# Packed-key products in float32 on 64-by-32 tiles, and weights kept in one float32

## Chip, cores and metric

The kernel runs on one core of one Trainium2 chip. The metric is the device time of one execution in microseconds (us).

## What is computed

Eight batches of eight heads pass through two softmax attentions (576 queries, 32 packed positions, head size 64), then two feed-forward layers follow on 4608 tokens. q, k, v and p are float32; all weight matrices are float64. Cut to what matters:

```python
def sm_attn(qq, kk, vv):                       # per batch and head
    s = scale * np.matmul(qq, kk.transpose(0, 1, 3, 2))
    s = s - np.max(s, axis=-1, keepdims=True)
    a = np.exp(s)
    a = a / (np.sum(a, axis=-1, keepdims=True) + 1e-09)
    return np.matmul(a, vv)
p_packed = sm_attn(p, k, v)                    # [8, 8, 32, 64]
out = sm_attn(q, p_packed, p_packed)           # [8, 8, 576, 64]
x = out.transpose(0, 2, 1, 3).reshape(4608, 512)
h = np.maximum(np.maximum(x @ w1, x @ w2), x @ w3)   # [4608, 768]
x = h @ w_out                                        # [4608, 512]
h = x @ w_in                                         # [4608, 2048]
P = a[0] + a[1] * h + a[2] * h**2 + a[3] * h**3
Q = 1.0 + abs(b[0]) * abs(h) + abs(b[1]) * h**2
result = (P / (Q + 1e-06)) @ w_out2                  # [4608, 512]
```

## The kernel before

**Stages.** Batches are worked in four pairs (`bp`). A pair has four units `u`: a batch (`b2`) and a group of four heads (`g`). For a unit, `s_stage` (S) multiplies p with k, `a_stage` and `v_stage` (T, V) form the packed values, `z_stage` (Z) transposes them into `ppk`, the packed keys. `s2_stage` (s) multiplies them with q; two later softmax steps (g) give `a2h` and `a2l`, the second attention's weights. The second attention's values meet w1, w2 and w3 first: `m_stage` (m) multiplies packed keys by a piece of these weights, and `y_stage` multiplies the result `mh`, `ml` by `a2h`, `a2l`, for each of six blocks `f` of 128 hidden columns and each of three weights `w`, and keeps the maximum `hm`, which becomes `hh`, `hl`. `x2_stage` multiplies these by `w_out` and stores x to HBM. When all four pairs are done, a last part (`h_mm`, `g_stage`, `o_mm`) does the rational layer in nine blocks of 512 tokens.

**High and low parts.** Most products are done as three fp32r products of high and low parts (`mm3`, lines 61 to 63). `split` (lines 51 to 58) casts to the high part on ACT and subtracts on DVE or POOL. The score products (lines 260 and 322) and those of line 363 are float32 products, each with 32 columns of the array, written to a quarter of PSUM's partitions; `pt` and `ppk` hold zeros in the rows of the other head, so that all 128 rows take part.

**Weights.** A float64 weight comes as two 32-bit words per element. `decode` takes it apart on DVE, ACT and POOL into `hi` and `lo`. `Feed` hands out the pieces: `step()` finishes the piece begun before, begins the next and loads a further one into `w_raw` (three buffers). 24 pieces of 384 columns (w1, w2, w3) and six of 512 (w_out) are decoded in START and in the first pair and stored to `w_scr`, from where `again` loads them for the later pairs. 32 pieces of 512 (`w_2`, for the last part) are decoded in pairs 1 to 3.

**Order.** `START` is a list written by hand for pair 0: each `|` ends a step, F is `feed.step()`, L, W and l load k, v and q. In `y_stage`, `between()` runs after each of the 36 groups of 12 products of a pair: it starts m stages of the next f, one step of `PACK` (the next pair's S, T, V, Z) and a feed step. `SECOND` runs between the x2 stages. A scheduler then places the instructions of each engine in an order of its own that follows the program's as its priority. All loads named here go through SyncE's queue, in order.

## Time and profile before

| | |
|---|---|
| median of 3 runs | 1428.18 us (1426.24 to 1429.65) |
| the profiled execution | 1429.64 us |
| its span, first to last instruction | 1427.9 us |
| mean granted TensorE clock | 0.973 |

The profile is of one execution. Busy time is the time in which an engine ran instructions; PEld is the weight load that overlaps PE's products. The granted clock is a share of full speed. A float32 product of 32 columns leaves two records in the profile (x16 for eight products). Matmul ends are modelled, so the distance from one start to the next is the safer measure.

### The profile page before, as it was taken

Reading aid. Unit: us, or ns where it says so; the run is one execution under the profiler, and the core shown is the slowest. Engines: PE = TensorE matmul, PEld = TensorE weight load, DVE = VectorE, ACT = ScalarE, POOL = GpSimd, SP = SyncE. Lnnn points to the kernel's source line nnn. Section 1 sums busy time; section 2 is a strip of 40 time slices with the busy share of each in tenths; the row PEclk is TensorE's granted clock in tenths of the full one; section 3 lists DMA queues with packets and bytes.
Section 4 is the critical chain, followed back from the end, with each engine's and each line's share of the span. In section 5 each row is a group of like instructions: output and inputs, shape, how many; then the busy total and the mean of one; then the engine's idle time right before and its main releaser. Section 6 shows DMA issues by size and latency. Waiting matters only on the chain.

```text
span 1427.9 us, 21290 instructions
## 1 busy us (share of the span) xinstructions
PE 1337.6 (94%) x8016; PEld 1140.2 (80%) x8016; DVE 1093.5 (77%) x1712; ACT 893.0 (63%) x1523; POOL 351.1 (25%) x350
## 2 busy tenths in 40 slices
PE   5468899998999899999999999999999999999998
PEld 2257799887988799998888888888888888888886
DVE  5999854668475848339897888978888888888887
ACT  4577743655355536337686766868677686676765
POOL 4676632447444555300010100101001010000000
PEclk9598999999999999999999999999999999999999
DMA  9757662768556645583010100101001010010000
GB/s 290 224 188 220 221 232 78 245 209 297 173 174 228 240 165 192 180 293 154 1 59 1 56 4 7 53 1 60 1 8 52 1 52 1 11 42 0 31 1 30
DMA packets 76743, 159.72 MB, mean 112 GB/s; under 512 B 11104, under 2 KB 35680, under 8 KB 75872
## 3 DMA queue, kind: packets, MB, share of 16 engines
q1 hardware_dynamic: 76352, 157.84, 33.0%
q8 instruction: 63, 1.03, 0.3%
q10 hardware_dynamic: 288, 0.52, 0.1%
q14 instruction: 40, 0.33, 0.1%
HBM read 113.25 MB, written 45.09 MB: 111 GB/s over the span
## 4 chain that ended last, share of the span: by engine, by line
PE 76%; DMA 7%; DVE 3%; ACT 2%; issue 1%; SPq 0%; POOL 0%; DVEq 0%; ACTq 0%; POOLq 0%
PE po L61 9%; PE po L63 9%; PE po L62 9%; PE psh L62 9%; PE psh L61 9%; PE psh L63 9%; PE psy L61 6%; PE psy L63 6%; PE psy L62 6%; DMA w_raw<-in_w_dram 3%; DMA wi_b<-w_scr 2%; DMA w_scr<-wt 1%; DVE wt L88 1%; PE pst L363 1%; DVE ml L58 1%
## 5 line engine op out<-in xcount | busy, mean ns | idle before, releaser
L619 ACT ACTIVATE hb<-psh,babs 128x512 f32<-128x512 f32 (+1 forms) x145 | 100.1, 690 | 190.0 <-PE psh L63 190.0
L61 PE MATMUL po<-wq_b,gh 128*128 128x512 f32 x540 | 212.3, 393 | 0.8 <-ACT gh L54 0.8
L62 PE MATMUL po<-wq_b,gh 128*128 128x512 f32 x540 | 211.3, 391 | 0.0
L61 PE MATMUL psy<-a2h,mh 128*128 128x288 f32 x576 | 179.9, 312 | 31.3 <-ACT hm L449 13.8
L62 PE MATMUL psh<-xl,wi_b 128*128 128x512 f32 x504 | 196.9, 391 | 0.0
L63 PE MATMUL psh<-xh,wi_b 128*128 128x512 f32 x504 | 196.6, 390 | 0.0
L61 PE MATMUL psh<-xh,wi_b 128*128 128x512 f32 x504 | 196.5, 390 | 0.0
L58 POOL TENSOR_TENSOR xl<-xr,xh 128x512 fp32r<-128x512 f32 x28 | 36.5, 1304 | 627.7 <-ACT xh L54 627.7
L622 DVE SCALAR_TENSOR_TENSOR hb<-h,babs,hb 128x512 f32<-128x512 f32 (+1 forms) x145 | 108.3, 747 | 98.1 <-ACT h L620 98.0
L63 PE MATMUL po<-wq_b,gl 128*128 128x512 f32 x540 | 181.7, 391 | 0.0
L63 PE MATMUL psy<-a2h,ml 128*128 128x288 f32 x576 | 173.3, 301 | 2.5 <-DVE ml L58 2.4
L62 PE MATMUL psy<-a2l,mh 128*128 128x288 f32 x576 | 172.8, 300 | 0.0
L61 PEld LDWEIGHTS psy<-a2h,mh 128*128 128x128 f32 x576 | 110.9, 193 | 43.2 <-ACT hm L449 17.2
L61 PE MATMUL psy<-hh,wo_h 128*128 128x288 f32 x384 | 115.9, 302 | 9.6 <-ACT hm L467 8.6
L63 PEld LDWEIGHTS po<-wq_b,gl 128*128 128x128 f32 x540 | 101.3, 188 | 24.0
L61 PEld LDWEIGHTS po<-wq_b,gh 128*128 128x128 f32 x540 | 101.4, 188 | 22.9 <-ACT gh L54 1.2
L62 PEld LDWEIGHTS po<-wq_b,gh 128*128 128x128 f32 x540 | 101.4, 188 | 22.5
L451 DVE TENSOR_TENSOR hm<-psy,hm 128x576 f32<-128x576 f32 x96 | 72.4, 754 | 58.3 <-PE psy L63 54.6
L63 PE MATMUL psy<-hh,wo_l 128*128 128x288 f32 x384 | 115.0, 299 | 0.0
L62 PE MATMUL psy<-hl,wo_h 128*128 128x288 f32 x384 | 114.9, 299 | 0.0
L621 ACT ACTIVATE u<-psh,av 128x512 f32<-128x512 f32 (+1 forms) x145 | 113.9, 785 | 1.6 <-DVE gl L58 1.6
L627 DVE SCALAR_TENSOR_TENSOR u<-u,av,h 128x512 f32<-128x512 f32 (+1 forms) x145 | 107.8, 743 | 8.3 <-ACT h L624 8.3
(114 smaller groups left out, 3203.4 us busy)
## 6 DMA issues: line engine op xcount, KB each, us to landing
wt<-w_scr SPq DMA_DIRECT2D x72, 384.0 KB, 4.4
w_raw<-in_w_dram SPq DMA_DIRECT2D x32, 512.0 KB, 5.0
w_scr<-wt SPq DMA_DIRECT2D x32, 512.0 KB, 4.3
kt<-in_k_dram SPq DMA_DIRECT2D x16, 576.0 KB, 5.2
vraw<-in_v_dram SPq DMA_DIRECT2D x16, 576.0 KB, 6.7
w_raw<-in_w_dram SPq DMA_DIRECT2D x24, 384.0 KB, 3.4
kt<-in_q_dram SPq DMA_DIRECT2D x16, 576.0 KB, 6.7
w_scr<-wt SPq DMA_DIRECT2D x24, 384.0 KB, 3.4
```

The lines of the kernel that those rows point to most:

```text
L58: e.tensor_tensor(out=lo, in0=src, in1=hi.bitcast(F32), op=ALU.subtract)
L61: pe.matmul(out_ap, lhsT=lh, rhs=rh, start=first, stop=False)
L62: pe.matmul(out_ap, lhsT=lh, rhs=rl, start=False, stop=False)
L63: pe.matmul(out_ap, lhsT=ll, rhs=rh, start=False, stop=last)
L88: dve.scalar_tensor_tensor(out=hib, in0=hw, scalar=-0x80000000, in1=t, op0=ALU.bitwise_and, op1=ALU.bitwise_or)
L363: pe.matmul(pv[32 * h : 32 * h + 32, :64], lhsT=at[:, 3 * i + cp, o : o + 32], rhs=vt[:, h, c, :], start=c == 0, stop=c == VC - 1)
L451: dve.tensor_tensor(out=hm, in0=ps[:, :, :288], in1=hm, op=ALU.max)
L619: act.activation(hb, h, AF.Abs, scale=babs[:, 0:1])
L621: act.activation(u, h, AF.Identity, scale=av[:, 3:4], bias=av[:, 2:3])
L622: dve.scalar_tensor_tensor(out=hb, in0=h2, scalar=babs[:, 1:2], in1=hb, op0=ALU.mult, op1=ALU.add)
L627: dve.scalar_tensor_tensor(out=u, in0=u, scalar=av[:, 0:1], in1=h2, op0=ALU.add, op1=ALU.mult)
```

## The change

- **m products.** `m_stage` no longer uses fp32r parts on 128 rows and 128 columns. Per head it issues one float32 product of 64 rows by 32 columns, 384 wide; eight per stage, with all three weights of a group of heads in one stage. The evacuation is one split of 128 partitions instead of two of 64. `pp` goes, and with it most of `z_stage`.
- **Scores.** Both score products take the 64 rows of their own head; the zeros go.
- **Weights.** Pieces of w1, w2, w3 are 768 wide, twelve in number, and are kept in one float32 (`single`). The low word is added on DVE instead of ACT and POOL, for all pieces. w_out comes as four pieces by its output columns. `half_step` does half of `step`; a piece is now loaded when another is finished, and Feed2 starts with three loaded.
- **Order.** START is rewritten, with six half steps and two softmax steps left for the y stage; `between` starts m stages one step later (2 and 4 of 6 instead of 1 and 3) and takes 22 half steps in pair 0; x2 runs over output blocks outside and batches inside. `hl` of pair 0 (and the last of each pair) is subtracted on DVE. The coefficients a and b are loaded in the last pair. The first block of the last part's weights has a tile of its own, `wi_0`, and the second moves to `wi_b`.

```diff
@@ -65,76 +65,90 @@
...
-    def decode(pl, raw, n):
+    def decode(pl, raw, n, single):
         hw, lw = raw[:, :, 1], raw[:, :, 0].bitcast(U32)
-        t = pl.tile([128, n], I32, name="dec_t", bufs=2)
-        r = pl.tile([128, n], I32, name="dec_r", bufs=2)
-        rf = r.bitcast(F32)
-        dve.tensor_scalar(out=t, in0=hw, scalar1=0x7FFFFE00, scalar2=None, op0=ALU.bitwise_and)
-        dve.tensor_scalar(out=r, in0=hw, scalar1=0x1FF, scalar2=None, op0=ALU.bitwise_and)
+        t = pl.tile([128, 768], I32, name="dec_t", bufs=2)[:, :n]
+        r = pl.tile([128, 768], I32, name="dec_r", bufs=1)[:, :n]
+        keep = 0x7FF00000 if single else 0x7FFFFE00
+        dve.tensor_scalar(out=t, in0=hw, scalar1=keep, scalar2=None, op0=ALU.bitwise_and)
+        if single:
+            dve.tensor_scalar(out=r, in0=hw, scalar1=0xFFFFF, scalar2=0x100000, op0=ALU.bitwise_and, op1=ALU.bitwise_or)
+        else:
+            dve.tensor_scalar(out=r, in0=hw, scalar1=0x1FF, scalar2=None, op0=ALU.bitwise_and)
         act.activation(t, t, AF.Relu, scale=8.0, bias=reb)
-        mixed = next(plans) == "m"
-        if mixed:
-            dve.scalar_tensor_tensor(out=rf, in0=lw, scalar=2.0**-32, in1=r, op0=ALU.mult, op1=ALU.add)
+        act.activation(r.bitcast(F32), r, AF.Copy, scale=2.0**-20)
+        hi, lo = yield
+        rf = lo if single else r.bitcast(F32)
+        dve.scalar_tensor_tensor(out=rf, in0=lw, scalar=2.0**-52, in1=r.bitcast(F32), op0=ALU.mult, op1=ALU.add)
+        hib = hi if hi is not None and hi.dtype == I32 else t
+        dve.scalar_tensor_tensor(out=hib, in0=hw, scalar=-0x80000000, in1=t, op0=ALU.bitwise_and, op1=ALU.bitwise_or)
+        if single:
+            w = t
         else:
-            l = raw[:, :, 0].bitcast(F32)
-            act.activation(l, lw, AF.Copy, scale=2.0**-52)
-            act.activation(rf, r, AF.Copy, scale=2.0**-20)
-            pool.tensor_tensor(out=rf, in0=rf, in1=l, op=ALU.add)
-        hi, lo = yield
-        hib = hi if hi.dtype == I32 else t
-        dve.scalar_tensor_tensor(out=hib, in0=hw, scalar=-0x80000000, in1=t, op0=ALU.bitwise_and, op1=ALU.bitwise_or)
-        w = pl.tile([128, n], I32, name="dec_w", bufs=1)
-        dve.tensor_scalar(out=w, in0=hib, scalar1=-0x00800000, scalar2=None, op0=ALU.bitwise_and)
-        if mixed:
-            dve.tensor_scalar(out=w.bitcast(F32), in0=w.bitcast(F32), scalar1=2.0**-20, scalar2=None, op0=ALU.mult)
-        if hib is t:
-            act.copy(hi, t.bitcast(F32))
+            w = hw
+            dve.tensor_scalar(out=w, in0=hib, scalar1=-0x00800000, scalar2=None, op0=ALU.bitwise_and)
+            if hib is t:
+                act.copy(hi, t.bitcast(F32))
         pool.tensor_tensor(out=lo, in0=rf, in1=w.bitcast(F32), op=ALU.mult)
...
     class Feed:
+        def __init__(self, pl, pieces, bufs, first=0):
             self.pl, self.pieces, self.bufs, self.raw, self.half = pl, iter(pieces), bufs, [], []
-            self.load()
+            for _ in range(first):
+                self.load()
-        def step(self):
+        def start(self):
+            if self.raw:
+                raw, piece = self.raw.pop(0)
+                gen = decode(self.pl, raw, raw.shape[1], piece[3]) if wide else None
+                if gen is not None:
+                    next(gen)
+                self.half.append((gen, raw, piece))
+        def finish(self):
             if self.half:
-                gen, raw, (tiles, _, then) = self.half.pop(0)
+                gen, raw, (tiles, _, then, single) = self.half.pop(0)
                 hi, lo = tiles()
...
                         pass
+                elif single:
+                    act.copy(lo, raw)
...
-            if self.raw:
-                raw, piece = self.raw.pop(0)
-                gen = decode(self.pl, raw, raw.shape[1]) if wide else None
-                if gen is not None:
-                    next(gen)
-                self.half.append((gen, raw, piece))
                 self.load()
+        def half_step(self):
+            if self.half:
+                self.finish()
+            else:
+                self.start()
+        def step(self):
+            self.finish()
+            self.start()
...
@@ -146,62 +160,66 @@
...
-    w_scr = dram.tile([6, NHP, 128, 2, 384], F32, name="w_scr")
+    w_scr = dram.tile([6, 2, 128, 768], F32, name="w_scr")
     w2_scr = dram.tile([128, 2, 32 * 512], F32, name="w2_scr")
...
-    wo_h = big_b.tile([128, 6, DM], F32R, name="wo_h")
-    wo_l = big_b.tile([128, 6, DM], F32R, name="wo_l")
+    wo_h = big_b.tile([128, 4, 768], F32R, name="wo_h")
+    wo_l = big_b.tile([128, 4, 768], F32R, name="wo_l")
...
-    wt_ready, NWT, NW = [], 4, 6 * NHP
+    def wt_tile():
+        return wp.tile([128, 2, 512], F32, name="wt", bufs=NWT)
+    def w_piece(f, g):
...
         def tiles():
-            box.append(wp.tile([128, 2, 512], F32R, name="wt", bufs=NWT)[:, :, :384])
-            wt_ready.append(box[0])
-            return box[0][:, 0, :], box[0][:, 1, :]
+            box.append(wt_tile().rearrange("p a b -> p (a b)")[:, :768])
+            wt_ready[2 * f + g] = box[0]
+            return None, box[0]
...
-            nc.sync.dma_start(w_scr[f, hp], box[0].bitcast(F32))
-        return tiles, w123[NHP * f + hp], keep
+            nc.sync.dma_start(w_scr[f, g], box[0])
+        return tiles, w123[2 * f + g], keep, True
...
     def next_wt():
-        n = next(used) + NWT
-        wt = wt_ready.pop(0)
+        n = next(used)
+        wt = wt_ready.pop(n)
+        n += NWT
         return wt, (n if NW <= n < NBP * NW else None)
...
     def again(n):
         if n is not None:
-            wt = wp.tile([128, 2, 512], F32R, name="wt", bufs=NWT)[:, :, :384]
-            nc.sync.dma_start(wt.bitcast(F32), w_scr[n // NHP % 6, HPS[n % NHP]])
-            wt_ready.append(wt)
+            wt = wt_tile().rearrange("p a b -> p (a b)")[:, :768]
+            nc.sync.dma_start(wt, w_scr[n // 2 % 6, n % 2])
+            wt_ready[n] = wt
...
     def wo_pieces():
-        for f in range(6):
-            yield (lambda f=f: (wo_h[:, f], wo_l[:, f])), w_out[f], None
+        for m in range(4):
+            yield (lambda m=m: (wo_h[:, m], wo_l[:, m])), w_out[m], None, False
...
-            yield tiles, w_2[i], keep
+            yield tiles, w_2[i], keep, False
...
@@ -237,15 +255,11 @@
...
-    ppk = a2p.tile([128, 4, 2, 128], F32, name="ppk")
-    NKT, NPT = 4, 3
-    pt = [kp.tile([128, 2, 128], F32, name=f"pt{i}") for i in range(NPT)]
+    ppk = a2p.tile([128, 2, 4, 128], F32, name="ppk")
+    pt = kp.tile([128, 4, 2, 64], F32, name="pt")
-    for t in pt:
-        dve.memset(t, 0.0)
-    pool.memset(ppk, 0.0)
-    pool.memset(pp2.bitcast(F32), 0.0)
...
@@ -256,9 +270,10 @@
         for c2 in range(2):
             for h in range(4):
-                x = 32 * (h ^ 2 * b2)
-                pe.matmul(ps[x : x + 32, c2, :288], lhsT=ppk[:, u % 4, c2, 32 * h : 32 * h + 32],
-                          rhs=qt[:, 288 * h : 288 * h + 288], start=True, stop=True)
+                x = 32 * (h ^ b2)
+                l = slice(64 * c2, 64 * c2 + 64)
+                pe.matmul(ps[x : x + 32, c2, :288], lhsT=ppk[l, u // 4 % 2, u % 4, 32 * h : 32 * h + 32],
+                          rhs=qt[l, 288 * h : 288 * h + 288], start=True, stop=True)
...
@@ -282,31 +297,29 @@
...
     def m_tiles(f):
-        return [[mp[f % 2].tile([128, 2, 384], F32R, name=f"m{x}", bufs=2) for x in "hl"] for b2 in range(2)]
-    def m_stage(bp, i, mt):
+        return [mp[f % 2].tile([128, 2, 2, 384], F32R, name=f"m{x}") for x in "hl"]
+    def m_stage(bp, g, mt):
         ps = ps_t.tile([128, 2, 512], F32, name="pst")
-        for g in range(2):
-            wt, n = next_wt()
-            lh, ll = (t[:, bp % 2, g, 2 * i : 2 * i + 2, :].rearrange("p a b -> p (a b)") for t in pp)
-            mm3(ps[:, g, :384], lh, ll, wt[:, 0, :], wt[:, 1, :], True, True)
-            again(n)
-        for half in range(2):
-            b2 = half if i == 0 else 1 - half
-            l = slice(64 * half, 64 * half + 64)
-            split(mt[b2][0][l], mt[b2][1][l], ps[l, :, :384])
-    def load_p(u):
+        wt, n = next_wt()
+        for b2 in range(2):
+            for h in range(4):
+                i, j = divmod(h, 2)
+                l, c = slice(64 * j, 64 * j + 64), 32 * (h ^ b2)
+                pe.matmul(ps[c : c + 32, b2, :384], lhsT=ppk[l, bp % 2, 2 * g + b2, 32 * h : 32 * h + 32],
+                          rhs=wt[l, 384 * i : 384 * i + 384], start=True, stop=True)
+        again(n)
+        split(*(t[:, :, g, :] for t in mt), ps[:, :, :384])
+    def load_p(bp):
         for c2 in range(2):
-            l = slice(64 * c2, 64 * c2 + 64)
-            nc.sync.dma_start(pt[u % NPT][l, :, l], p[place(u)])
+            nc.sync.dma_start(pt[64 * c2 : 64 * c2 + 64], p[bp])
...
@@ -315,12 +328,14 @@
     def s_stage(u, kt):
         ps = ps_y.tile([128, 2, 512], F32, name="psy")
         for i in range(2):
-            for x in range(4):
-                l, c = 32 * x, 288 * (2 * i + x % 2)
-                pe.matmul(ps[l : l + 32, i, :288], lhsT=pt[u % NPT][:, i, l : l + 32], rhs=kt[:, c : c + 288],
-                          start=True, stop=True)
+            for c2 in range(2):
+                for j in range(2):
+                    l, x, c = slice(64 * c2, 64 * c2 + 64), 64 * (c2 ^ i) + 32 * j, 288 * (2 * i + j)
+                    pe.matmul(ps[x : x + 32, i, :288], lhsT=pt[l, u % 4, i, 32 * j : 32 * j + 32], rhs=kt[l, c : c + 288],
+                              start=True, stop=True)
...
@@ -370,17 +385,9 @@
     def z_stage(u):
-        n, b2 = divmod(u, 2)
-        bp, g = divmod(n, 2)
         ps = ps_t.tile([128, 2, 512], F32, name="pst")[:, 0]
         pe.transpose(ps[:, :128], zt[u % 2].rearrange("p a b -> p (a b)"), ident)
-        sl = slice(0, 4, 3) if b2 == 0 else slice(1, 3)
-        for j in range(2):
-            l = slice(64 * j, 64 * j + 64)
-            copy = act.copy if j == 0 else dve.tensor_copy
-            copy(ppk[l, u % 4, j, :], ps[l, :128])
-            split(*(t[l, bp % 2, g, sl, 32 * j : 32 * j + 32] for t in pp),
-                  ppk[l, u % 4, j].rearrange("p (i j x) -> p i j x", i=2, j=2)[:, :, j, :], lo_eng="pool")
+        act.copy(ppk[:, u // 4 % 2, u % 4, :], ps[:, :128])
...
@@ -395,9 +402,12 @@
...
-                feed.step()
+                feed.half_step()
+            elif k == "R":
+                feed.load()
+            elif k == "P":
+                load_p(self.bp)
-                load_p(u)
                 self.kt[i] = load_unit(kk, u)
...
@@ -461,7 +471,7 @@
...
-                mm3(ps[:, half, :288], wo_h[:, f, 128 * m : 128 * m + 128], wo_l[:, f, 128 * m : 128 * m + 128],
+                mm3(ps[:, half, :288], wo_h[:, m, 128 * f : 128 * f + 128], wo_l[:, m, 128 * f : 128 * f + 128],
...
@@ -488,23 +498,15 @@
...
-    pieces = [w_piece(0, hp) for hp in HPS] + wo[:3]
-    for f in range(1, 6):
-        pieces += [w_piece(f, hp) for hp in HPS] + wo[f + 2 : f + 3]
+    ws = [w_piece(f, g) for f in range(6) for g in range(2)]
+    pieces = ws + wo
-    for x in "L0 L1 W0".split():
+    feed = Feed(wp, pieces, NRAW)
+    for x in "P L0 L1 W0 R W1 L2 L3 R".split():
         ahead.do(x)
-    feed = Feed(wp, pieces, bufs=NRAW)
-    nc.sync.dma_start(av, a_in.partition_broadcast(128))
-    nc.sync.dma_start(bv, b_in.partition_broadcast(128))
-    START = ("S0 L2|S1 W1|T0 F|L3|V0 S2|T1 F|Z0 W2|V1 S3|T2 F|Z1 W3|V2 l0|T3 F|Z2 l1|V3 F|Z3 l2|s0 F|g s1 m0 l3|F g s2|"
-             "g s3 m1 F|g F|g F")
+    START = ("S0|S1|T0|T1|V0 W2|Z0 F|V1 l0 W3|Z1 F|S2 l2|S3 l1|m0 F|T2 l3|T3 R|F V2|Z2|s0|V3|g Z3|s2 F|g m1|s1|g s3 F")
     for _ in ahead.steps(START):
...
@@ -514,12 +516,19 @@
...
-            feed2 = Feed(wp, w2_pieces(), bufs=NRAW)
+            feed2 = Feed(wp, w2_pieces(), NRAW, NRAW)
...
         if bp + 1 < NBP:
-            for x in "L0 W0 L1 W1".split():
+            for x in "P L0 W0 L1 W1".split():
...
@@ -528,33 +537,39 @@
...
-            def between(bp=bp, f=f):
+            def between(bp=bp, f=f, now=now):
                 t = next(turn)
-                if f < 5 and t % 6 in (1, 3):
-                    m_stage(bp, t % 6 // 2, nmt)
+                if now.soft:
+                    now.do("g")
+                if f < 5 and t % 6 in (2, 4):
+                    m_stage(bp, t % 6 // 2 - 1, nmt)
                 if t >= 2:
                     next(pack, None)
                 if bp == 0:
-                    feed.step()
+                    if t % 3 < 2 and t < 32:
+                        feed.half_step()
                 elif t in y_steps[bp]:
                     feed2.step()
...
             for b2 in range(2):
-                hs[b2][f] = y_stage(b2, f, mt[b2], a2[b2], between)
+                hs[b2][f] = y_stage(b2, f, [t[:, b2] for t in mt], a2[b2], between,
+                                    "dve" if bp == 0 or (b2, f) == (1, 5) else "pool")
...
+            for m in range(4):
+                for b2 in range(2):
+                    x2_stage(2 * bp + b2, m, hs[b2])
+                    next(gen, None)
+                    if bp == 0:
+                        feed.half_step()
+                    if 2 * m + b2 in windows[bp]:
+                        feed2.step()
-            for b2 in range(2):
-                for m in range(4):
-                    x2_stage(2 * bp + b2, m, hs[b2])
-                    next(gen, None)
-                    if 4 * b2 + m in windows[bp]:
-                        feed2.step()
```

## Rows read from the trace of the kernel before

**Rows 1.** The page's first part: busy time, share of the span.

```profile
PE 1337.6 (94%) x8016; PEld 1140.2 (80%) x8016; DVE 1093.5 (77%) x1712; ACT 893.0 (63%) x1523; POOL 351.1 (25%) x350
```

**Rows 2.** Stretches: length; busy PE, PEld, DVE, ACT, POOL; clock; DMA; GB/s.

```profile
0.00:65.87 65.87, 30.39 (x361) 16.47 (x361) 48.82 (x103) 32.89 (x71) 36.34 (x57) 0.76 0.84 265
65.87:187.53 121.66, 97.32 (x788) 85.78 (x789) 104.31 (x169) 85.85 (x167) 78.82 (x83) 0.89 0.62 200
187.53:234.50 46.97, 46.62 (x372) 43.15 (x372) 24.58 (x41) 16.84 (x26) 19.07 (x15) 1.00 0.57 193
234.50:326.70 92.20, 84.63 (x772) 76.45 (x771) 59.31 (x99) 51.03 (x94) 40.34 (x48) 0.98 0.62 204
326.70:380.80 54.10, 49.70 (x371) 45.88 (x372) 37.22 (x60) 25.27 (x40) 36.05 (x26) 0.94 0.76 261
...
525.60:591.40 65.80, 64.37 (x471) 63.69 (x470) 45.72 (x60) 33.58 (x50) 29.88 (x21) 1.00 0.39 133
...
630.90:1427.90 797.00, 792.07 (x3456) 648.58 (x3456) 670.91 (x1019) 564.48 (x934) 36.53 (x28) 1.00 0.09 32
```

**Rows 3.** The same table for the 30 us from 120.

```profile
120.00:150.00 30.00, 23.37 (x207) 20.95 (x206) 27.50 (x47) 23.95 (x48) 20.87 (x23) 1.00 0.67 218
```

**Rows 4.** Groups by line and shape in the first y stretch, DVE, then ACT.

```profile
L58 DVE TENSOR_TENSOR ml<-pst,mh 64x768 fp32r<-64x768 f32 x22 | 21.0, 953 | 1.6 <-ACT mh L54 1.2
L451 DVE TENSOR_TENSOR hm<-psy,hm 128x576 f32<-128x576 f32 x24 | 18.1, 753 | 8.4 <-PE psy L63 8.1
L88 DVE SCALAR_TENSOR_TENSOR dec_t<-w_raw,dec_t 128x384 int32<-128x384 int32 x19 | 16.6, 879 | 0.1
L75 DVE TENSOR_SCALAR dec_t<-w_raw 128x384 int32<-128x384 int32 x18 | 11.7, 650 | 0.1
L76 DVE TENSOR_SCALAR dec_r<-w_raw 128x384 int32<-128x384 int32 x18 | 11.1, 616 | 0.9 <-POOL wt L95 0.9
...
L327 DVE TENSOR_SCALAR mx<-mx 64x2 f32<-64x2 f32 x8 | 5.1, 634 | 0.2
...
L54 ACT CAST mh<-pst 64x768 fp32r<-64x768 f32 x20 | 15.9, 793 | 2.6 <-DVE ml L58 2.1 <-PE pst L63 0.2
```

**Rows 5.** Waits of PE from 234.5 to 525.6: total us, times, longest.

```profile
PE psy L61 <- ACT hm L449: 10.0, 8, 2.6
```

**Rows 6.** The chain in order of time, from 275 us: start, us, what.

```profile
276.68 6.37 DMA w_raw<-in_w_dram
283.07 0.65 ACT w_raw L83
283.72 0.54 ACT hm L449
```

**Rows 7.** Timeline of PE in the first x2 stretch, around one score stage.

```profile
192.16 0.29 PE L63 MATMUL psy<-hh,wo_l 128*128 128x288 f32 x1
192.38 1.18 PE L260 MATMUL psy<-kt,ppk 128*32 128x288 f32 x16
...
193.77 0.34 PE L62 MATMUL pst<-wt,pp 128*128 128x384 f32 x1
...
195.53 0.34 PE L63 MATMUL pst<-wt,pp 128*128 128x384 f32 x1
```

**Rows 8.** Timeline of PE in START: one score stage, one value stage.

```profile
32.52 1.18 PE L260 MATMUL psy<-kt,ppk 128*32 128x288 f32 x16 [1.25 <-ACT ppk L381]
33.51 0.86 PE L363 MATMUL pst<-vraw,at 96*32 96x64 f32 x48
```

**Rows 9.** Groups by line over the span: count, busy us, mean ns.

```profile
L260 PE MATMUL psy<-kt,ppk 128*32 128x288 f32 x256 | 22.9, 457 | 5.3 <-ACT ppk L381 3.0 <-DVE ppk L381 2.3
```

**Rows 10.** Single lines over the span: shortest, median, longest in ns.

```profile
L75 DVE TENSOR_SCALAR dec_t<-w_raw x62: 341/420/1590, 11.7 to 566.6; 128x512 int32<-128x512 int32 x38, 128x384 int32<-128x384 int32 x24
...
L80 DVE SCALAR_TENSOR_TENSOR dec_r<-w_raw,dec_r x5: 494/559/1036, 21.3 to 70.3; 128x384 f32<-128x384 uint32 x4, 128x512 f32<-128x512 uint32 x1
...
L88 DVE SCALAR_TENSOR_TENSOR dec_t<-w_raw,dec_t x30: 532/586/1782, 15.6 to 162.7; 128x384 int32<-128x384 int32 x24, 128x512 int32<-128x512 int32 x6
```

More of the change, by code (lines that the diff above doesn't have):

```diff
@@ L95, in decode, with load_raw @@
         pool.tensor_tensor(out=lo, in0=rf, in1=w.bitcast(F32), op=ALU.mult)
-    def load_raw(pl, src, bufs=2):
+    def load_raw(pl, src, bufs):
         n = src.shape[1]
-        raw = pl.tile([128, n, 2] if wide else [128, n], I32 if wide else F32, name="w_raw", bufs=bufs)
+        raw = pl.tile([128, 768, 2] if wide else [128, 768], I32 if wide else F32, name="w_raw", bufs=bufs)[:, :n]
         nc.sync.dma_start(raw.rearrange("p n w -> p (n w)") if wide else raw, src.bitcast(I32) if wide else src)
@@ L162, in attn_moe_moe2_kernel @@
     rlow = ctx.enter_context(tc.tile_pool(name="rlow", bufs=1, side="right"))
-    pp2 = rlow.tile([128, 2, 2, 2, 4, 64], F32R, name="pp2")
-    pp = [pp2[:, x] for x in range(2)]
+    wi_0 = rlow.tile([128, 2, 512], F32R, name="wi_0")
     rstack = ExitStack()
@@ L454, in y_stage @@
         hl = hp_pool.tile([128, S], F32R, name=f"hl{b2}{f}")
-        split(hh, hl, hm.rearrange("p a b -> p (a b)"), lo_eng="pool")
+        split(hh, hl, hm.rearrange("p a b -> p (a b)"), lo_eng=lo_eng)
         return hh, hl
```

35 lines of the change are left out of this document (18 added, 17 removed).

## The prediction

> **What bounds the kernel now.** I read the page's busy shares first. TensorE is busy 94% of the span [rows 1], but that is a mean over unlike stages, so the next view is a table of stretches, cut where the y products (lines 61 to 63 into psy from a2h), the x2 products and the last layer begin and end [rows 2]. It shows three regimes. From 630.9 to the end, 797 us, the last layer keeps PE busy 792.1 us at full clock; of this the diff moves only where two weight blocks lie. In the middle (234.5 to 591.4) PE is busy about 92% and leads; each pair of batches costs some 92 us of y and some 54 us of x2. Before that, PE does not lead: in START (0 to 65.87) it is busy 30 of 66 us while the DMA engines are at 0.84 and DVE at 49 us, and in the first y stretch (121.66 us for products that take 65.80 in the last one) DVE is busy 104.3, POOL 78.8, and the granted clock is 0.89. In the 30 us from 120 on DVE is at 92% [rows 3]. So up to 187 us the bound is the decoding of the float64 weights (bytes first, then DVE), and after it PE with what it waits for.
>
> What DVE does there is in its groups for that stretch [rows 4]: 21.0 us of ml, 18.1 of the running maximum hm, and the decode, 39.4 us in the three groups shown (sign, mask, mask of the 384-wide pieces).
>
> For PE's waits the list of the two middle pairs is led by an ACT copy, hm L449, with 10.0 us [rows 5]. ACT is not slow there: the chain shows the copy standing in ACT's order behind the cast of a raw weight piece, which waits 6.37 us for its DMA [rows 6]. Feed holds one piece ahead, and SyncE's queue issues it late. Four such waits for w_raw stand in that chain between 276 and 346 us.
>
> **The m products (48 stages).** Now six fp32r products per stage, at 0.176 us each (ten steps from 193.77 to 195.53 [rows 7]): 1.06 us. They become eight float32 products of 64 rows by 32 columns, 384 wide. Float32 products of 32 columns are in the trace, with all rows used. Eight of 288 columns take 1.18 us and 24 of 64 columns 0.86 us [rows 8]: 0.32 us for 768 product-columns more, so 0.22 us plus 0.417 ns per product-column. Eight of 384 at this rate are 1.50 us; if the two row halves run at once as well, 0.22 + 0.64 = 0.86. A change of shape costs more than the row: from 192.16 to 193.77 are 1.61 us [rows 7], in which the score stage stands beside one product of each ordinary kind (0.13 and 0.18), so the stage takes 1.30, 0.12 above its row. So a stage costs 0.98 or 1.62, against 1.06: from -4 to +27 us over 48. I take 0.98, because products on different columns already overlap (256 records of 457 ns fill 22.9 us [rows 9]), and the eight tiles of a stage are eight different pairs of a row half and a column quarter.
>
> The Trainium skill (TensorE: Matmul & The Clock Gate, Part 3: Packing small matmuls — row/col tiling) says that tiles of different row and column groups run at the same time, and gives 10.6 times for sixteen of them. By it a stage would be 0.98 and the sum 1365 rather than 1404; no row here has two row groups in use, so the trace can't confirm it.
>
> **Scores (32 stages).** The same eight tiles, 288 wide: 1.30 becomes 0.22 + 0.48 + 0.12 = 0.82, or stays. I take 0.82.
>
> **Splits and packed keys.** m's split comes as one 128x768 instruction on ACT and on DVE instead of two of 64 rows; 953 ns goes with the 768 elements per row [rows 4], so DVE saves 0.95 us per stage. But the second stage of an f is issued after step 4 of 6 where it was after step 3, so that one step of 12 products, 1.6 us, and the first products of the next f (0.7 us until ml of g=1 is used) cover its two instructions, 0.79 on ACT and 0.95 us on DVE [rows 4], with some 0.2 between engines: 1.95 of 2.3. One hm (0.75) ahead of it on DVE and PE waits 0.4 us: 5 times in each y, 2 us, hidden in the first, where DVE leads. The casts and subtractions of pp go; they were on ACT and POOL and hidden. The memsets at the start go, hidden by the first DMA.
>
> **Decode, and the first y stretch.** A w piece is now 768 wide, with four DVE instructions (two masks, the add, the sign) in place of eight of 384, two ACT instead of eight, one POOL instead of four. One such piece costs DVE at most twice the shortest 384 times, 2 x (0.341 + 0.34 + 0.494 + 0.532) = 3.4 [rows 10] (the second mask by the first), and at worst twice the means of the crowded stretch, 2 x (0.65 + 0.62 + 0.49 + 0.88) = 5.3 [rows 4]. The gap between shortest and mean appears while POOL is 65% busy; POOL now loses three of four decode instructions and the hl subtractions, so I estimate it at a third. I take 3.9, near the low end. The stretch has 22 half steps, 11 pieces: 43; one more mask for the two w_out pieces 1.5; ml 10 x 0.95 = 9.5; hm 18; hl moved from POOL to DVE 12 x 0.75 (an hm instruction's size) = 9; the next pair's scores and keys about 10 (half of it the 64x2 row); softmax left over from START 4. That is 95 us instead of 104, and at the 92% of [rows 3] 104 us instead of 121.66. PE's own work, some 80, stays below it. Bounds: 84 (pieces at 3.4, PE leads) and 122.
>
> **START.** It moved 265 GB/s x 65.87 us = 17.5 MB [rows 2]. The new order loads before the first y product p (256 KB), twelve tiles of k, q and v of 576 KB, five raw pieces of 768 KB instead of about a dozen of 384 or 512, and stores two of 384: 12.1 MB, 46 us at the same rate. DVE's share falls from 49 to some 33 us (three pieces instead of eleven, two softmax left for later), so bytes lead. Bounds: 34 us (8.9 MB strictly needed) and 66. I take 46.
>
> **The middle.** Feed2 starts with three pieces loaded and fetches the next when one is finished, two steps earlier than now, so most of the stops of [rows 6] go. Its DVE cost is a further add per piece, 0.6 us x 32 [rows 10], hidden: DVE is at 64 to 69% there [rows 2]. A w2 piece's raw buffer is now held until POOL's product, which delays the load queued on SyncE by some 2 us, covered by the depth. y: PE busy 84.6 less 10 x 0.08 and 4 x 0.48 = 81.9, plus a third of the 7.6 idle: 84, and 2 for the later m stage: 86 instead of 92.2. x2: the undisturbed one is 46.97, less 4 x 0.48 + 2 x 0.08 = 2.1, plus 2: 47 instead of 54.1. The next pair (380.8 to 525.6, 144.8 us) the same, 133. In the last y stretch -0.8 and the 2: +1.2. x2's new order needs w_out's columns one block at a time, which only moves the last decode; the first x2 stretch gives 45 instead of 47.
>
> **Sum.** -19.9 (START) - 17.7 (y) - 2 (x2) - 6.2 - 7.1 (second pair) - 11.8 (third) + 1.2 = -63.5. The profiled execution took 1429.64 us, 1.74 outside its span: 1366.1. It lies 1.46 above the median of the runs, so in their terms 1365.
>
> **Rivals.**
> *Four tiles at a time.* Halving the rows brings no overlap: m stages 1.62, scores 1.30. For: no row shows row halves. Against the forecast this adds 8.3 to each middle y, 3.2 to each of three x2, 6.4 to the last y and some 6 under DVE's cover in front: 39, so 1404, still faster.
> *The front does not shrink.* DVE pieces stay at 5.3 us: y at 121, START at 55 because the chain from first score to first y is serial. For: DVE's instructions are fewer, not less work. Against: POOL's load halves. 1391.
> *One row half at a time in a bank.* In the m stages and the scores of p both row halves write the same PSUM bank. If they can't do so together, only two tiles overlap: m 0.22 + 2.56 + 0.12 = 2.90, those scores 2.26. That is 48 x 1.92 + 16 x 1.44 = 115 more than forecast: 1480, slower than before. It decides from an m stage of 2.0 us on, where 60 times the excess (48 stages, and 16 score stages at three quarters of it) eats 63.5. Against: columns differ, so no two tiles write the same partitions.
> The Trainium skill (TensorEngine Tiling (Array Packing), Gotcha 1: PSUM Pressure) states such a rule: different row tiles can't access one PSUM bank at the same time. No row here tests it.
>
> **Chances.** Forecast 0.58, with its own range 1345 to 1384 (y between 97 and 112, START 40 to 52, PE's waits in the middle all gone or half kept); four at a time 0.22; front 0.14; bank 0.06. The first three lie about or under 1404, so the range is 1338 to 1405, with about 0.08 below and 0.12 above. Faster by over 0.2% (what the runs here can tell from nothing) 0.93, within it 0.01, slower 0.06.
>
> **What the next profile shows.** An m stage: a row of 16 records near 0.86 us (right), 1.5 or 2.8. First y product at 46 us, first x2 at 150, the last layer from about 567 for 797 us. ACT's copies no longer behind raw pieces. DVE's add under 1.3 us. It would be wrong if DVE's decode instructions are as long per element as now, or if PE waits for w_raw as before.

## The result and the profile after

The changed kernel takes 1392.49 us (median of 4 runs, 1391.14 to 1393.72) where the kernel before took 1428.91 beside it: a ratio of 0.9747, with a 95% interval from 0.973 to 0.9765. Its profiled execution has a span of 1391.8 us against 1427.90, so the spans differ by 36.1 us. The forecast was 63.5 less.

The page's first part (busy time, share of the span, instructions):

```profile
PE 1313.8 (94%) x8496; PEld 1091.5 (78%) x8496; DVE 1051.1 (76%) x1630; ACT 802.2 (58%) x1337; POOL 242.7 (17%) x230
```

PE's share is the 94% of [rows 1]: the mean tells nothing here either. The table of stretches, cut at the same events as [rows 2] (START, y, x2, y, x2, y, x2, y, last layer; columns as there):

```profile
0.00:53.98 53.98, 25.70 (x380) 12.27 (x381) 31.85 (x63) 20.96 (x40) 19.93 (x34) 0.81 0.98 316
53.98:172.20 118.22, 94.38 (x919) 74.31 (x919) 95.69 (x136) 57.27 (x93) 38.99 (x36) 0.86 0.53 170
172.20:215.75 43.55, 43.16 (x380) 39.71 (x375) 18.91 (x33) 11.21 (x18) 14.92 (x12) 1.00 0.39 130
215.75:298.68 82.93, 80.64 (x893) 67.05 (x891) 53.74 (x93) 38.23 (x71) 29.79 (x34) 1.00 0.59 187
298.68:350.30 51.62, 46.21 (x377) 42.73 (x371) 37.94 (x64) 18.61 (x30) 24.77 (x18) 0.93 0.75 256
350.30:434.03 83.73, 80.74 (x892) 67.09 (x890) 54.84 (x93) 38.21 (x71) 29.51 (x34) 1.00 0.50 162
434.03:487.45 53.42, 47.09 (x410) 42.66 (x403) 41.92 (x69) 20.41 (x32) 25.89 (x19) 0.94 0.72 237
487.45:554.44 66.99, 65.40 (x531) 58.95 (x529) 38.29 (x53) 24.58 (x38) 22.31 (x16) 1.00 0.21 72
...
594.95:1391.80 796.85, 792.10 (x3456) 648.64 (x3456) 670.86 (x1019) 564.54 (x934) 36.56 (x28) 1.00 0.09 32
```

Against [rows 2] the stretches changed by (forecast in brackets): START -11.9 (-19.9), first y -3.4 (-17.7), first x2 -3.4 (-2), second y -9.3 (-6.2), second x2 -2.5 (-7.1), third y with its x2 -7.7 (-11.8), last y +1.2 (+1.2), last x2 +1.0 (none), last layer -0.2 (none). So 22 of the 27 us that are missing are missing ahead of the first x2 product.

The timeline of PE in the changed kernel shows the new products, a stage in each row (start, length, the records of its eight products):

```profile
23.91 0.72 PE L337 MATMUL psy<-kt,pt 64*32 64x288 f32 x16
...
26.74 0.72 PE L275 MATMUL psy<-kt,ppk 64*32 64x288 f32 x16 [0.60 <-ACT ppk L390]
...
54.54 0.88 PE L313 MATMUL pst<-wt,ppk 64*32 64x384 f32 x16
```

The scores went from the 1.18 of [rows 7, 8] to 0.72 (0.70 without the shape change was forecast), an m stage is 0.88 (0.86). With its changes of shape an m stage costs 1.01: from 500.06 to 501.33 in PE's timeline, less two ordinary steps of 0.13 (0.98 was forecast). These prices are right.

### The profile page after: what moved, and what is told of

Its sections match the earlier page's. It is cut to its first block, busy times and chain, and to the rows that moved or that the text cites. A ratio compares the mean times of both kernels' runs of the same rounds, so it can differ in the third digit from the quotient of the medians.

```text
span 1391.8 us, 21572 instructions
## 1 busy us (share of the span) xinstructions
PE 1313.8 (94%) x8496; PEld 1091.5 (78%) x8496; DVE 1051.1 (76%) x1630; ACT 802.2 (58%) x1337; POOL 242.7 (17%) x230
## 4 chain that ended last, share of the span: by engine, by line
PE 81%; DVE 5%; DMA 4%; ACT 2%; issue 1%; POOL 1%; SPq 0%; ACTq 0%; POOLq 0%; DVEq 0%
PE po L61 10%; PE po L62 9%; PE po L63 9%; PE psh L62 9%; PE psh L61 9%; PE psh L63 9%; PE psy L61 8%; PE psy L62 7%; PE psy L63 7%; PE pst L313 2%; DMA wi_b<-w_scr 1%; DMA w_raw<-in_w_dram 1%; DMA x_scr<-hm 1%; PE pst L378 1%; DVE wt L87 1%
## 5 line engine op out<-in xcount | busy, mean ns | idle before, releaser
L62 PE MATMUL psh<-xl,wi_b 128*128 128x512 f32 x540 | 211.0, 391 | 0.0
L63 PE MATMUL psh<-xh,wi_b 128*128 128x512 f32 x540 | 210.6, 390 | 0.0
L61 PE MATMUL psh<-xh,wi_b 128*128 128x512 f32 x540 | 210.6, 390 | 0.0
L61 PE MATMUL psy<-a2h,mh 128*128 128x288 f32 x576 | 181.6, 316 | 17.1 <-DVE hm L461 8.1
L61 PE MATMUL psy<-hh,wo_h 128*128 128x288 f32 x384 | 117.2, 305 | 12.1 <-ACT hm L477 11.7
L461 DVE TENSOR_TENSOR hm<-psy,hm 128x576 f32<-128x576 f32 x96 | 72.4, 754 | 63.2 <-PE psy L63 60.3
L61 PEld LDWEIGHTS psh<-xh,wi_b 128*128 128x128 f32 x540 | 101.4, 188 | 22.1
L62 PEld LDWEIGHTS psh<-xl,wi_b 128*128 128x128 f32 x540 | 101.4, 188 | 21.7
L63 PEld LDWEIGHTS psh<-xh,wi_b 128*128 128x128 f32 x540 | 101.4, 188 | 21.7
```

The source lines that it names most:

```text
L61: pe.matmul(out_ap, lhsT=lh, rhs=rh, start=first, stop=False)
L62: pe.matmul(out_ap, lhsT=lh, rhs=rl, start=False, stop=False)
L63: pe.matmul(out_ap, lhsT=ll, rhs=rh, start=False, stop=last)
L461: dve.tensor_tensor(out=hm, in0=ps[:, :, :288], in1=hm, op=ALU.max)
```

## The experiments

Each run was timed beside the kernel before; the ratio of the changed kernel, 0.9747, is the reference. Four kernels whose code is the same up to the first x2 product (the changed one, `e2`, `e5`, `e10`) reach that product between 167.8 and 172.2 us, so a smaller difference in front says nothing.

**Row halves.** All products of the packed keys on one half of the rows (`e1`):

```
-  l, c = slice(64 * j, 64 * j + 64), 32 * (h ^ b2)
+  l, c = slice(0, 64), 32 * (h ^ b2)          # scores likewise
```

> The products of the packed keys (scores and m) read rows 0 to 63 of the array for both halves, so the second half's numbers are computed from the first half's rows; the number, the size and the column groups of the products stay. Theory (row halves run at once): an m stage goes from the 0.88 us of the changed kernel's timeline to 1.50 or more, a score stage from 0.72 to about 1.18, and the time rises by 48 x 0.62 + 32 x 0.46 = 44 us, less what DVE hides in front: about 39 over the 1392 of the changed kernel, near 1431. Rival (the gain is that of the column quarters, and the halves add nothing): the rows and the time stay, within 3 us.

Ratio 0.9939 (0.9915 to 0.9962). Timeline of PE in `e1`, an m stage and a score stage of p:

```profile
523.42 1.49 PE L313 MATMUL pst<-wt,ppk 64*32 64x384 f32 x16
...
103.49 1.18 PE L337 MATMUL psy<-kt,pt 64*32 64x288 f32 x16
```

These are the forecast's two prices for four tiles at a time (1.50 and 1.18), so the halves do overlap in the changed kernel. The span is 24.4 us longer, not 44: the second y stretch pays in full (+8.6), the third 6.3, START and first y 6.1 together, the x2 stretches between -0.9 and +1.9, and the last y 2.1, where only six of the stages stand (the trace has 96 records) and 1.4 us of PE's waiting went into them. By the ratios, 0.0192 of 1427, it is 27.

**Depth of w2's fetch** (`e2`; w2 is here the last part's `w_2`): `step` loads one piece after `start`, and `Feed` begins with one piece instead of three.

```
-  feed2 = Feed(wp, w2_pieces(), NRAW, NRAW)
+  feed2 = Feed(wp, w2_pieces(), NRAW, 1)      # and load() in step, not in finish
```

> w2's raw pieces are fetched one ahead, as in the kernel before, instead of three; nothing else differs. Theory (the depth of the fetch is what freed the second and third pair: y 92.2 to 82.9 and 91.5 to 83.7, x2 54.1 to 51.6): the waits for raw pieces come back and the time rises by 10 to 15 us. Rival (narrower splits, the gathered ACT instructions and cheaper products freed them): within 3 us of the changed kernel.

Ratio 0.9742 (0.9724 to 0.9759); the second y and x2 take 82.93 and 51.59 us, as in the changed kernel. The depth alone is worth nothing that can be measured.

**Load order in START** (`e3`):

```
-  for x in "P L0 L1 W0 R W1 L2 L3 R".split():
+  for x in "P L0 L1 W0 L2 W1 L3 R R".split():  # and no third R in START
```

> At the start the tiles that the scores of z need are loaded ahead of the second and third raw weight piece (tiles 2 and 3 before, raw pieces behind, two instead of three before the last of them). Theory (PE's first wait, 6.7 us for the third score tile, is the order of the loads, and the first y product hangs on it): the first y product comes 5 us or more earlier and the time falls by 4 to 7 us. Rival (DVE's softmax and decode chain sets y's density, whatever comes first): first product earlier or not, the first x2 product within 2 us of now and the time within 3 us; slower if the decode of the first piece is later.

Ratio 0.9734 (0.9709 to 0.9758): not told apart from the changed kernel. The first y product came 1.2 us earlier, the first x2 product at 167.7, the lower edge of what equal code gives. The third score tile did come 5.7 us earlier (13.89 instead of 19.56), but nothing behind it: the theory's 5 us are not there.

**Less work on DVE in front** (`e4`): one decode instruction less for each piece of w1 to w3.

```
+  if single: rf = r.bitcast(F32)               # the low word is left out
+  else:
       dve.scalar_tensor_tensor(out=rf, in0=lw, scalar=2.0**-52, in1=r.bitcast(F32), ...)
```

> The low word of the twelve pieces of w1 to w3 is left out of the weights, and with it one DVE instruction per piece (0.97 us): the kernel computes with less precise weights; loads, stores and order stay. Theory (DVE bounds the front until 172 us): 12 us of DVE go, 8 of them before the last of them is used, and the first x2 product comes 6 to 10 us earlier. Rival (bytes and order of the front bound it, DVE only in parts of it): 0 to 4 us.

Ratio 0.969 (0.9673 to 0.9707), and the first x2 product at 160.5 instead of 172.2, more than the 6 to 10 us of the theory.

**hl back on POOL** (`e6`):

```
-  "dve" if bp == 0 or (b2, f) == (1, 5) else "pool")
+  "dve" if (b2, f) == (1, 5) else "pool")
```

> The low parts hl of the first pair are subtracted on POOL again, as in the kernel before, instead of on DVE. Theory (DVE bounds the first y stretch, one for one as the 12 us left out showed): 11 x 0.75 = 8 us of DVE go and the first x2 product comes 6 to 8 us earlier. Rival (DVE's instructions become longer while POOL works, which is why the prediction gave the change POOL's relief): the means of DVE's decode rise by some 10% and the first x2 product comes within 2 us of now.

Ratio 0.9727 (0.9714 to 0.974), first x2 product at 168.8: at most a small gain, not told apart.

**The add back on POOL** (`e8`):

```
-  dve.scalar_tensor_tensor(out=rf, in0=lw, scalar=2.0**-52, in1=r.bitcast(F32), ...)
+  act.activation(l, lw, AF.Copy, scale=2.0**-52)
+  pool.tensor_tensor(out=rf, in0=r.bitcast(F32), in1=l, op=ALU.add)
```

> The two words of a weight are added on POOL again, with the low word made float by one more ACT instruction, instead of in one DVE instruction; the width of the pieces, the order and everything else stay. Theory (DVE bounds the front, and POOL at a third has room): 12 x 0.97 us of DVE go, and the first x2 product comes 6 to 10 us earlier, as where the low word was left out; in the second and third x2 stretch DVE's busy time falls by 2 us and they by 1 to 2. Rival (POOL's work lengthens DVE's instructions and delays the pieces, which is what the change bought itself out of): DVE's masks get longer by 10% or more and the time stays within 3 us or rises.

Ratio 0.9783 (0.9768 to 0.9798), first x2 product at 173.1: slower than the changed kernel by some 5 us. By the spans it is 4.8 us, of which 0.9 are ahead of the first x2 product; the second y and x2 stretch, where w2's pieces are decoded in the same way, are 3.1 and 2.2 longer, and the third pair gives 1.9 back. The 30 us behind the first y product tell the three apart. The table of stretches for them, the changed kernel:

```profile
54.00:84.00 30.00, 12.40 (x89) 8.31 (x90) 29.08 (x40) 13.29 (x18) 19.01 (x12) 0.68 0.64 219
```

The same for `e4`:

```profile
53.40:83.40 30.00, 18.21 (x137) 13.08 (x134) 20.46 (x31) 12.39 (x20) 16.32 (x14) 0.83 0.74 258
```

The same for `e6`:

```profile
51.70:81.70 30.00, 12.22 (x88) 8.13 (x88) 29.09 (x38) 13.29 (x18) 19.95 (x13) 0.68 0.69 238
```

The same for `e8`:

```profile
55.20:85.20 30.00, 14.85 (x101) 10.36 (x101) 27.60 (x37) 17.71 (x27) 25.27 (x18) 0.65 0.62 213
```

In the changed kernel DVE (third busy time) is full there and PE does 12 us of work. `e4` opens it. `e6` takes 8.5 us from DVE over the whole stretch (87.19 for 95.67), but only one of the twelve hl instructions stands in these 30 us (at 81.75), so they stay full. In `e8` POOL's busy time rises from 38.98 to 62.18 in the first y, and DVE's other instructions get longer. In `e6` it rises nearly as far, to 57.22, and on the whole they do not: the 8.5 us that DVE gains are all of hl's 8.2, the mean of the second mask (L78) falls from 855 to 623 ns and that of the sign (L87) rises from 1257 to 1378. So POOL's busy time alone is not the cause; the section below shows what is. Groups of DVE in the first y, in the changed kernel (count, busy us, mean ns):

```profile
L58 DVE TENSOR_TENSOR hl<-hm,hh 128x576 fp32r<-128x576 f32 x11 | 8.2, 748 | 0.0
...
L78 DVE TENSOR_SCALAR dec_r<-w_raw 128x768 int32<-128x768 int32 x6 | 5.1, 855 | 0.0
...
L76 DVE TENSOR_SCALAR dec_t<-w_raw 128x512 int32<-128x512 int32 x2 | 3.1, 1559 | 1.2 <-DMA w_raw<-in_w_dram 1.2
```

The same groups in `e8`:

```profile
L58 DVE TENSOR_TENSOR hl<-hm,hh 128x576 fp32r<-128x576 f32 x11 | 10.9, 992 | 2.6 <-ACT hh L54 2.6
...
L78 DVE TENSOR_SCALAR dec_r<-w_raw 128x768 int32<-128x768 int32 x6 | 8.4, 1402 | 0.0
L76 DVE TENSOR_SCALAR dec_t<-w_raw 128x512 int32<-128x512 int32 x2 | 4.1, 2064 | 0.0
```

Of the 10.6 us of the eleven adds in that stretch (6.8 and 3.8), DVE got only 3.5 back (92.13 for 95.67).

**More bytes** (`e12`), behind START's first loads:

```
+  for i in range(2):
+      nc.sync.dma_start(w2_scr[:, i, :1536].bitcast(I32), w123[i].bitcast(I32))
```

> Two more copies of 768 KB (1.57 MB read, and written to a scratch that is overwritten later) are issued behind the first loads; nothing reads them in front. At the start's 316 GB/s that is 5.0 us of the DMA engines. Theory (bytes bound the front up to the first y products): the third score tile and the first dense y products come some 5 us later and the first x2 product 4 to 6 us later. Rival (DVE's softmax and decoding set when y becomes dense, and the transfers run ahead of need): first x2 product within 2 us and the time within 3 us.

Ratio 0.9751 (0.9729 to 0.9773). The first y product came 2.9 us later, the first x2 product at 170.4, and from 24 to 84 us DVE is as busy as without the copies (53.28 and 52.99 us). Here the transfers run ahead of need.

**Place of the m stages** (`e7`), and with w2's steps moved as well (`e9`):

```
-  if f < 5 and t % 6 in (2, 4): m_stage(bp, t % 6 // 2 - 1, nmt)
+  if f < 5 and t % 6 in (1, 3): m_stage(bp, t % 6 // 2, nmt)
-  y_steps = {1: range(1, 36, 4), ...}          # e9 only, all three pairs
+  y_steps = {1: range(2, 36, 4), ...}
```

> Each m stage is issued one step of products earlier, the second of an f after step 3 of 6 as in the kernel before. The prediction's price for the later place was 2 us in each of the three later y stretches and nothing in the first. By it: 6 us less. Rival (the later place cost nothing visible, since the splits were on time): within 2 us.

> The m stages at their earlier place, as in the run that issued them one step earlier, and w2's steps moved by one step of products as well (t = 2, 6, 10 .. instead of 1, 5, 9 ..), so that no step of products issues both. Theory (what the later place gains is that m's split and w2's decoding no longer stand in the same step on DVE and ACT): the second and third y stretch come back from 89.2 and 89.5 to within 2 us of the changed kernel's 82.9 and 83.7, and the time within 5 us of it, 1392. Rival (the later place itself gains, by what it has behind it): they stay at 88 or more and the time near 1405.

`e7`: ratio 0.9838 (0.9825 to 0.9852), 13 us slower than the changed kernel; the second, third and last y are 89.2, 89.5 and 68.4 us. `e9`: 0.9855 (0.9832 to 0.9877), with 87.1 and 87.4. For `e7` the theory and the rival both fell: the later place gains. For `e9` the theory fell and the rival came close: some two of the six us in each y go with the coincidence with w2's steps. The total of `e9` is no lower than that of `e7`, since its first x2 product came 4.0 us later (171.3 and 167.3). PE's waits over the two middle pairs (the second y to the third x2) in the changed kernel, as in [rows 5] (total us, times, longest):

```profile
PE psy L61 <- ACT hm L477: 11.7, 5, 5.3
...
PE psy L61 <- DVE hm L461: 0.4, 2, 0.2
```

The same in `e7`:

```profile
PE psy L61 <- ACT hm L477: 13.4, 4, 5.4
PE psy L61 <- DVE hm L461: 10.8, 8, 2.6
...
PE psy L61 <- ACT hm L459: 1.3, 2, 0.7
```

L461 is the running maximum. One of the longest of its waits, in the timeline of `e7` (rows of DVE and POOL): PE has run out of work at 255.22, and the maximum that frees its buffer stands behind the decode and a tiny instruction of the next pair's scores (L344). That one takes 1.24 us, as it ends only with POOL's product, at 257.03; the longest wait of the third y, 2.55 us before 400.54, looks the same.

```profile
254.04 0.68 DVE L87 SCALAR_TENSOR_TENSOR wt<-w_raw,dec_t 128x512 int32<-128x512 int32 x1
254.75 0.34 DVE L342 TENSOR_SCALAR mx<-mx 64x2 f32<-64x2 f32 x2
255.12 0.43 DVE L92 TENSOR_SCALAR w_raw<-wt 128x512 int32<-128x512 int32 x1
255.47 0.42 DVE L76 TENSOR_SCALAR dec_t<-w_raw 128x512 int32<-128x512 int32 x1
255.69 1.34 POOL L95 TENSOR_TENSOR wt<-dec_r,w_raw 128x512 fp32r<-128x512 f32 x1 [3.77 <-DVE w_raw L92]
255.80 1.24 DVE L344 SCALAR_TENSOR_TENSOR mx<-mx 128x2 f32<-128x2 f32 x1
256.97 0.74 DVE L461 TENSOR_TENSOR hm<-psy,hm 128x576 f32<-128x576 f32 x1
```

In the changed kernel no POOL instruction runs beside L344, which takes 0.16 us, and the same maximum stands ahead of the decode; DVE is idle for 0.38 us before it and starts it when its products end:

```profile
256.77 0.16 DVE L344 SCALAR_TENSOR_TENSOR mx<-mx 128x2 f32<-128x2 f32 x1
257.31 0.76 DVE L461 TENSOR_TENSOR hm<-psy,hm 128x576 f32<-128x576 f32 x1 [0.38 <-PE psy L63]
...
258.96 0.69 DVE L87 SCALAR_TENSOR_TENSOR wt<-w_raw,dec_t 128x512 int32<-128x512 int32 x1
```

**w2's steps out of x2**, on every third step of y (`e5`), and on odd steps only, where no m stage is issued (`e10`):

```
-  y_steps = {1: range(1, 36, 4), 2: range(1, 36, 4), 3: range(1, 32, 4)}
-  windows = (), (0, 2, 4, 6), (1, 3, 5)
+  y_steps = {1: [*range(1, 36, 3), 35], 2: range(1, 36, 3), 3: range(1, 32, 4)}   # e5
+  y_steps = {1: (1, 3, 5, 9, 11, 13, 17, 21, 25, 27, 29, 33, 35), ...}            # e10
+  windows = (), (), ()
```

> The seven steps of w2's decoding that stand in the second and third x2 stretch are moved into the y stretches of the same pairs (13 and 12 steps instead of 9 and 9). Theory (the x2 products wait for ACT's copies, which stand behind the raw weights' instructions and their DMAs): the second and third x2 stretch fall from 51.6 and 53.4 us to about 46, the y stretches keep their 83 and 84 because DVE has room there, and the time falls by 8 to 12 us below the 1392 of the changed kernel. Rival (the next pair's keys and softmax, which stand there as well, hold the copies): x2 stays above 50 and the time within 3 us. Third possibility: the steps cost in y what they save in x2, sum within 3 us.

> As the run that moved w2's seven steps out of the x2 stretches, with the same 13 and 12 steps in y, but only in odd steps of products, where no m stage is issued; there 5 of 13 and 6 of 12 fell on a step with one. Theory (falling together with an m stage is what cost 12.8 and 5.6 us there): the y stretches fall from 95.7 and 89.3 to at most 88 and 86. Rival (a piece costs y some 3 us wherever it stands, since its transfers or its DVE time are the limit): 93 or more and 88 or more. For x2: near 46 in both if the seven steps were the stall, above 50 if it is the next pair's softmax or pieces that are late.

`e5`: 0.9818 (0.9805 to 0.9831), y 95.7 and 89.3, x2 51.3 and 51.1: 10 us slower than the changed kernel, which none of the three expectations said, though x2 stays above 50 as in the rival. `e10`: 0.9759 (0.9736 to 0.9781), y 89.0 and 87.8, x2 48.0 and 48.0. So with the steps that avoid the m stages (in `e5` five of the 13 and five, not six, of the 12 met one) y is 6.7 and 1.5 us shorter, and the stretches end up between the two expectations; what `e10` saves in x2 (9.0 us) it pays in y (10.2). The table of stretches for the second x2, `e5`:

```profile
307.02:358.32 51.30, 46.24 (x377) 42.75 (x371) 31.11 (x54) 16.43 (x26) 20.17 (x16) 0.93 0.61 217
```

The same for `e10`:

```profile
304.60:352.60 48.00, 44.51 (x377) 41.02 (x371) 31.06 (x54) 16.09 (x26) 21.39 (x16) 0.96 0.67 232
```

DVE has the same work there in both, 31.1 us, and still decodes: four or five instructions of each kind of w2's decode, where the changed kernel has six or seven. The steps left the list, but not all of their instructions left the stretch.

**Key tiles first and hl on POOL together** (`e11`: the edits of `e3` and `e6`).

> The load order with the key tiles first and hl of the first pair on POOL, together. If the small gains of the two alone add up (by their medians 2 and 3 us below the changed kernel): 1387 to 1389, ratio to the kernel before 0.971 to 0.972. If they were chance, or the one takes the other's room: 1390 to 1393, ratio 0.974 or 0.975.

Ratio 0.9746 (0.9727 to 0.9766): the small gains did not add up, as the expectation has it for chance. No complete kernel of these is measurably faster than the changed one.

## Why the prediction was right in direction and too large

**Row halves: right, shown.** m stages and scores cost what the forecast said, and `e1` shows the rival's price on the chip. The Trainium skill (TensorE: Matmul & The Clock Gate, Part 3: Packing small matmuls — row/col tiling) has tiles of different row and column groups run at the same time; the trace agrees: 0.88 us against 1.49 on one half. With the halves apart, the changed kernel would take some 27 us more, where the forecast's arithmetic said 39.

**One row half at a time in a bank: refuted.** In the m stages and the scores of p both halves write the same bank, in the scores of q each has its own; the two score stages both take 0.72, and the m stage is 0.88, not 2.78. The rule of the Trainium skill (TensorEngine Tiling (Array Packing), Gotcha 1: PSUM Pressure), that different row tiles can't access one bank at the same time, is not borne out for tiles that write different partitions of one bank.

**The first y stretch: the step that failed.** DVE's sums were right: it is busy 31.85 us in START (33) and 95.69 in y (95), and an early piece costs 3.95 (3.9: means 0.867, 0.855, 0.969 and 1.257). Part of that is luck: START decoded six pieces and not three, the softmax left over took 8.9 us of y and not 4, and the durations in y add up to 102.5 us, of which the overlap of neighbours takes off 7. The division by 0.92 was wrong: it took the 30 us of [rows 3] for the whole stretch, and DVE's share is 81% (86% in the kernel before: 104.31 of 121.66). Its three parts behind the first 30 us shown above, in the table of stretches of the changed kernel:

```profile
84.00:132.00 48.00, 46.66 (x479) 37.16 (x480) 31.19 (x50) 23.03 (x42) 8.61 (x16) 0.95 0.44 140
132.00:150.00 18.00, 14.05 (x135) 10.38 (x135) 17.62 (x23) 8.98 (x14) 5.99 (x3) 0.72 0.66 213
150.00:172.00 22.00, 21.06 (x225) 18.43 (x217) 17.77 (x25) 11.77 (x21) 5.36 (x6) 1.00 0.44 136
```

DVE is full for 48 us, PE for the other 70; the bound changes three times, and the work that `e6` spared DVE, nine of eleven instructions of it while PE led, gave nothing that could be measured. On PE's side: the second y, with much the same products, keeps PE busy 80.64 us, the first 94.38 (the forecast put PE's own work at some 80), and it stands idle 23.84. The 13.7 more are products at the lower level, 1.2 GHz, by an estimate from its granted clock (0.86 x 94.38 = 81). The timeline of PE shows some after a wait: the step from product to product is 0.24 us, at full clock 0.13.

```profile
141.35 0.61 PE L61 MATMUL psy<-a2h,mh 128*128 128x288 f32 x1 [2.49 <-DVE hm L461]
141.76 0.44 PE L62 MATMUL psy<-a2l,mh 128*128 128x288 f32 x1
142.00 0.44 PE L63 MATMUL psy<-a2h,ml 128*128 128x288 f32 x1
```

A part that DVE fills costs twice, then, in the wait and in the slower products after it. `e4` agrees: 18 us less of DVE in the first y gave 11 us, with PE's busy time down by 3.1. Only 6.8 of the 18 us are adds left out there; most of the rest is one sign instruction fewer, and decode instructions that POOL held up less (the sign's mean falls from 1257 to 958 ns).

**START: mis-sized by 8 us, and the wrong end.** It moved 17.1 MB (316 GB/s x 53.98), not 12.1: eight raw pieces and 17 tiles (five of them of the next pair) were issued and five pieces stored by then, pulled ahead of their place in the code. But bytes don't set the front, as `e12` shows, nor does the first y product mark its end: y is dense from about 84 us on. START and first y have to be priced as one: 172.2 us against 187.5, forecast 150. The rival in which the front does not shrink gave nearly these times (55, 121, 1391) by a wrong cause: it had pieces of 5.3 us, and they take 3.95.

**POOL's relief: right, but not by its busy share.** The gap between shortest and mean durations on DVE was put down to POOL's work, and a lower busy share was to close it. `e8` fits (855 to 1402 ns as POOL's busy time goes from 39 to 62 us), `e6` does not (39 to 57 us, and 623 ns). What counts is whether a POOL instruction is running when a mask starts. Two masks in the timeline of the changed kernel (rows of L76 and POOL):

```profile
135.98 0.55 DVE L76 TENSOR_SCALAR dec_t<-w_raw 128x768 int32<-128x768 int32 x1
137.50 1.83 POOL L95 TENSOR_TENSOR wo_l<-dec_r,w_raw 128x768 fp32r<-128x768 f32 x1 [3.19 <-DVE dec_r L85]
137.99 1.77 DVE L76 TENSOR_SCALAR dec_t<-w_raw 128x768 int32<-128x768 int32 x1
```

The second ends 0.4 us after POOL's product. Of the 19 masks of 768 columns that start in this y (L76, L78, L80), eleven start with no POOL instruction running and take 0.50 to 0.56 us. Eight start under one, and each ends 0.42 us after that one's end, which makes 0.57 to 2.19 us. In `e8` twelve of the 19 start under one, in `e6` eight, in `e4` four. The running maximum (L461) takes 0.74 to 0.77 us either way. `e8` also shows what the move of the add to DVE is worth: some 5 us of the total, little of it in front.

**The middle y: ACT's stops went as forecast, the cause stays open.** ACT's copies in y, 10.0 us of PE's waits in [rows 5], no longer stand in the list. But the cause that was named, the deeper fetch, isn't needed (`e2`), and with the cast of the raw words back on ACT the same wait is 0.7 us over the two pairs (`e8`). So neither is needed while the other stands. Both undone together wasn't run, and the narrower splits and fewer ACT instructions, the rival of `e2`, are in all of these kernels: which of them freed the copies stays open. The price of the later m stage had the wrong sign: +2 us a stretch forecast, -6 measured in the second and third y and -1.4 in the last (`e7`). At the earlier place the waits for ACT are gone too (1.3 us), but 10.8 us of waits for DVE's maximum take their place. What the forecast left out is DVE's order: a split issued one step earlier shifts what the maximum finds ahead of it, and what POOL runs just then. Why the queue comes out so well at the later place is only partly settled, since `e9` gives 2 of the 6 us to the steps of w2. PE's busy time fell by 4.0 of the 9.3 us (84.63 to 80.64), 2.7 of it forecast.

**x2: wrong.** Its copies wait as before: 11.7 us in the rows of the changed kernel above, against 8.3 in the list of [rows 5]:

```profile
PE psy L61 <- ACT hm L467: 8.3, 3, 4.4
```

The chain of the changed kernel in the second x2 stretch (start, length, what):

```profile
325.48 4.32 DMA w_scr<-wt
329.81 0.15 ACT dec_t L81
329.96 0.57 ACT e L285
330.54 0.53 ACT hm L477
```

The pattern of [rows 6] is still there: the copy stands behind a decode instruction, held by a transfer, here the store that frees a weight tile, and behind the next pair's exponential. The forecast read the pattern in y and took it to be one with x2's. DVE does more there than before (41.92 us in the third x2). In `e10` the two stretches fall from 51.6 and 53.4 to 48.0 (the first x2 takes 43.6), but `e5` moves the same seven steps and leaves 51.3 and 51.1. So the seven steps are not shown to be the stall, and moving them gains nothing; what holds the copies stays open.

## What to carry to other kernels

Where two engines take turns as the bound, do not divide one engine's work by one share: cut the stretch where the lead changes, and count a saving only where that engine leads. An instruction's place in an in-order queue can be worth more than its length, so a moved step needs its neighbours listed on every engine that it touches. A first product is not the start of dense work.
